# The places of the second layer's input tiles in a scheduled attention and two-layer kernel

## The chip, the cores and the metric

The kernel runs on one core of one Trainium2 chip. The metric is device time in microseconds (us) of one execution. A core has five engines that work side by side, each from its own queue of instructions: TensorE multiplies matrices into PSUM banks, VectorE and ScalarE work element by element, GpSimd is hardly used here, and SyncE (SP) issues the transfers (DMAs) between the chip's memory and SBUF. An instruction whose input is not there yet waits at the head of its engine's queue.

## The reference

Attention over 4 batches, 8 heads, 576 positions and 64 dimensions comes first: half of the heads look at the last 32 positions, the other half at every fourth of the last 128. Its output, put together as 2304 tokens of 512 numbers, goes through two layers without bias, in float32 (each layer has its own weights, 512 x 2048 and 2048 x 512; all four are taken as float64):

```
x = attention(q, k, v)                          # 2304 x 512
h = x @ moe_w_in;  x = (h * sigmoid(1.702 * h)) @ moe_w_out
h = x @ moe2_w_in; r = max(h, 0); out = (r * r) @ moe2_w_out
```

## The kernel before, in words

Tokens lie along the free dimension of a tile, features along its 128 partitions. Every float32 operand of a layer is split into a high part, rounded to float32r, and a low part, the rest; a product is three matmuls (high by high, high by low, low by high).

The tokens are worked off in blocks: six in the first layer (512, 256, 384, 512, 256, 384 columns, `sizes1`), five in the second (512, 256, 512, 512, 512, `BLOCKS2` at line 61). For each block, `step` runs 16 steps f, one for each 128 hidden features. A step has 12 matmuls into a bank h (lines 581 to 583, four pieces k of the input x), the activation (first layer lines 605 to 623; second layer a ReLU on ScalarE, line 633, and a square on VectorE, line 636), the split of its result g into gh (a cast, line 643, on ScalarE or VectorE) and gl (a subtraction on VectorE, line 647), and 12 matmuls into four output banks o (lines 667 to 669). After the last step the banks are evicted (line 690) and stored (line 697), the first layer's into a scratch tensor x2d in the chip's memory.

The input tile of a block holds high and low part of its 512 features. In the first layer it is written by the attention, into one of three places x0, x1, x2 by turns (x0 for blocks 0 and 3, x1 for 1 and 4, x2 for 2 and 5); x1 has room for 256 columns. In the second layer each block's input is filled from x2d (lines 811 to 832): four loads of one piece each (line 817) into a ring of three buffers raw2, and for each piece a cast into the high half (line 823, ScalarE or VectorE) and a subtraction into the low half (line 826, VectorE). These tiles lie in place x0 or in a further place xx, opened when the attention's buffers are given up. A raw2 buffer comes free with its piece's subtraction. In the trace tiles of x0, x1 and x2 have the name x, raw and raw2 buffers the name raw, and copies and subtractions stand at the helpers' lines 234, 236 and 245.

The weights of both layers come as float64 and are turned into split float32 by a chain on ScalarE and VectorE (lines 289 to 318). Each has one place, so the second layer's are made while the first layer's last block runs, step by step as it gives the first layer's up.

The order of all this is written by a planner, the class `Schedule` (lines 64 to 181), when the kernel is built. It holds a cost for every task, plans a start for each, and hands out tasks in the order of these starts; each engine's queue is then fixed, whatever the real times are. A task can start when its predecessors are done, its engine is free and its buffers have a place; at equal start the smaller due time (`want`) goes first (line 143). The place is asked for only as long as no earlier task has taken it for the same buffer:

```
for b in t["bufs"]:
    if not b["held"]:
        ...
        start = max(start, sorted(self.places[c])[k])
...
key = (max(start, free[e] + 0.02) + worse, t["want"], t["n"])
```

Line 158's filling matmuls aside, nothing keeps TensorE running when its next input is late. Due times of the second layer: a block begins where the one before it ends by the planner's costs (lines 743 to 746), step f is due f step lengths later, and piece k of a block's fill is due 60 - 10 k planner's us before the block begins (line 828).

Of the kernel before, what the change touches and what calls it, by code (L numbers as in the profile page):

```python
# [9 lines left out]
F32R = mybir.dt.float32r  # L10
# [7 lines left out]
P = 128  # L18
# [4 lines left out]
KD = DM // P  # L23
# [40 lines left out]
class Schedule:  # L64
# [18 lines left out]
    def buffer(self, cls):  # L83
        return {"cls": cls, "held": False, "left": 0, "end": 0.0}

    def task(self, engine, cost, want, fn, after=(), bufs=(), port=False):


        many = isinstance(engine, tuple)
        t = {  # L90
            "ways": dict(zip(engine, cost)) if many else {engine: cost}, "many": many,
            "want": want, "fn": fn, "bufs": bufs, "port": port,
            "left": 0, "ready": [], "next": [], "n": len(self.tasks), "end": None,
        }
        for a in after:
            a["next"].append(t)
            t["left"] += 1
        for b in bufs:
            b["left"] += 1
        self.tasks.append(t)  # L100
        return t
# [83 lines left out]
def attention_mlp_mlp(  # L185
# [46 lines left out]
    def copy(e, out, in_):  # L232
        if e == "act":
            A.copy(out, in_)  # L234
        else:
            by_name[e].tensor_copy(out, in_)
# [7 lines left out]
    def minus(e, out, a, b):  # L244
        by_name[e].tensor_tensor(out=out, in0=a, in1=b, op=ALU.subtract)  # L245


    def copies(n):
        return ("act", "dve"), (0.19 + n / 1536, 0.068 + n / 1920)
# [4 lines left out]
    def pairs(n):  # L254
        return ("dve",), (0.069 + n / 960,)
# [20 lines left out]
    def weights(layer, f, part, want):  # L276
# [46 lines left out]
        t = task("dve", 0.602, want - LEAD[1], top, [t], [raw_b, c_b], True)  # L323
        t = task("dve", 0.602, want - LEAD[1], low, [t], [raw_b, c_b], True)
        hi = task(*copies(DM), want - LEAD[2], high_part, [t], [c_b, w_b], True)
        lo = task(*pairs(DM), want - LEAD[2], low_part, [hi], [c_b, w_b], True)
        split_task[layer, f, part] = [hi, lo]
# [235 lines left out]
    def step(layer, blk, f, want, a=0, z=None):  # L563
# [81 lines left out]
        def low_part(e):  # L645
            m["gl"] = gpool.tile([P, 512], F32R, tag="gl", name="gl")[:, 0:n]
            minus(e, m["gl"], m["g"], m["gh"])

        hi = task(*copies(n), want, high_part, [last], [g_b, gh_b], True)
        lo = task(*pairs(n), want, low_part, [hi], [g_b, gh_b, gl_b], True)  # L650
        if f == 0:
# [101 lines left out]
    for b in range(1, B):  # L753
# [4 lines left out]
        blk = att_blocks[b - 1]  # L758
# [13 lines left out]
    def step_len(size):  # L772
        return 24 * mm(size)
# [6 lines left out]
    for n, size in enumerate(sizes1):  # L780
        blk = {
            "i": n, "n": size, "c0": sum(sizes1[:n]), "buf": x_buf[n],
            "x": lambda n=n: x_t[n], "ready": lambda k, n=n: x_done[n, k],
        }
# [15 lines left out]
    for n, size in enumerate(BLOCKS2):  # L800
        c0 = sum(BLOCKS2[:n])
        want = begin2[n]
        cls = ("xx", "x0")[n % 2]
        blk = {"i": n, "n": size, "c0": c0, "buf": buffer(cls), "done": {}}
        blk["x"] = lambda blk=blk: blk["tile"]
        blk["ready"] = lambda k, blk=blk: blk["done"][k]
        need = [
            i for i, size1 in enumerate(sizes1)
            if sum(sizes1[:i]) < c0 + size and sum(sizes1[:i]) + size1 > c0
        ]  # L810
        for k in range(KD):
            raw_b = buffer("raw2")
            m = {}

            def load(k=k, c0=c0, size=size, m=m):
                m["raw"] = close["pool"].tile([P, 512], F32, tag="raw2", bufs=3, name="raw2")[:, 0:size]
                nc.sync.dma_start(m["raw"], x2d[k, :, c0:c0 + size])

            def high_part(e, k=k, size=size, m=m, blk=blk, cls=cls):
                if "tile" not in blk:  # L820
                    pool = close["pool"] if cls == "xx" else xpool
                    blk["tile"] = pool.tile([P, 2, KD, 512], F32R, tag=cls, name=cls)
                copy(e, blk["tile"][:, 0, k, 0:size], m["raw"])

            def low_part(e, k=k, size=size, m=m, blk=blk):
                minus(e, blk["tile"][:, 1, k, 0:size], m["raw"], blk["tile"][:, 0, k, 0:size])

            w = want - 60 + 10 * k
            t = task("dma", size * 0.00142, w - 6, load, [stored[0, i, k] for i in need] + [reopened], [raw_b])
            t1 = task(*copies(size), w, high_part, [t], [raw_b, blk["buf"]], True)  # L830
            t2 = task(*pairs(size), w, low_part, [t1], [raw_b, blk["buf"]], True)
            blk["done"][k] = [t1, t2]
        for f in range(KF):
            w = want + step_len(size) * f
            if n == len(BLOCKS2) - 1 and f == KF - 1 and size == 512:

                step(1, blk, f, w, 0, size // 2)
                step(1, blk, f, w + step_len(size // 2), size // 2, size)
            else:
                step(1, blk, f, w)  # L840
# [88 lines left out]
```

## Time and profile before

| | us |
|---|---|
| median of 3 runs | 914.81 (912.86 to 916.9) |
| the profiled execution | 917.75 |
| its span, first to last instruction | 915.9 |
| TensorE busy in it | 890.4 |
| VectorE busy | 553.1 |
| ScalarE busy | 449.6 |

Times inside a trace count from the span's start. The profiled execution is one of its own, so a sum over the trace is made against its 917.75 us. Busy times of TensorE are modelled; its idle times and the starts of its matmuls show where it stood. The second layer begins at about 503 us.

### The profile page before, as it was taken

To read this page: it belongs to the slowest core of one execution; us is meant where nothing else is said; L and a number is where in the kernel's file an instruction comes from. 1 tells how busy PE (TensorE), PEld (TensorE's weight loads), DVE (VectorE), ACT (ScalarE), POOL (GpSimd) and SP (SyncE) were. 2 spreads that over 40 slices of the span, in tenths; PEclk is the share of its full clock that TensorE was granted. 3 is DMA by queue.
4 is the path that set the end of the run, shared out by engine and by line. 5 is a ranking of instruction groups with operands and counts; after the bars stand their busy time and mean duration, and the time that the engine had idled before them with its cause. 6 is when DMAs were issued, how large, how long until landed. Compare 5 with 4: busy or idle time off the path is not lost.

```text
span 915.9 us, 14046 instructions
## 1 busy us (share of the span) xinstructions
PE 890.4 (97%) x5149; PEld 761.0 (83%) x5149; DVE 553.1 (60%) x1542; ACT 449.6 (49%) x1224; POOL 1.2 (0%) x7
## 2 busy tenths in 40 slices
PE   7999999999999999999999999989999999999998
PEld 4677767999988777799999778879888888888887
DVE  6999999766688877764799982232322242222223
ACT  7999898573556555543566642222322232222222
POOL 0000000000000000000000000000000000000000
PEclk9999999999999999999999999989999999999999
DMA  6554445411112110130144520020200010001001
GB/s 232 176 183 158 168 141 169 138 29 40 38 46 79 46 45 23 35 116 1 70 160 146 179 103 0 1 93 1 70 0 1 1 58 1 0 1 46 1 1 46
DMA packets 28117, 65.08 MB, mean 71 GB/s; under 512 B 3121, under 2 KB 10801, under 8 KB 28049
## 3 DMA queue, kind: packets, MB, share of 16 engines
q1 hardware_dynamic: 28048, 64.20, 21.1%
q8 instruction: 40, 0.66, 0.3%
q14 instruction: 29, 0.23, 0.1%
HBM read 54.75 MB, written 9.44 MB: 70 GB/s over the span
## 4 chain that ended last, share of the span: by engine, by line
PE 78%; ACT 9%; DVE 8%; DMA 3%; issue 1%; SPq 0%; ACTq 0%; DVEq 0%
PE o L667 13%; PE o L669 13%; PE o L668 13%; PE h L581 13%; PE h L583 12%; PE h L582 12%; DMA raw<-in_w 2%; ACT sm L468 2%; ACT sm L240 2%; PE s L445 2%; PE pv L537 1%; DVE c L307 1%; ACT c L240 1%; DVE wl L245 1%; DVE c L301 1%
## 5 line engine op out<-in xcount | busy, mean ns | idle before, releaser
L667 PE MATMUL o<-gh,wh 128*128 128x512 f32 (+2 forms) x704 | 250.7, 356 | 6.7 <-ACT gh L234 4.6
L668 PE MATMUL o<-gh,wl 128*128 128x512 f32 (+2 forms) x704 | 248.4, 353 | 1.0 <-DVE wl L245 1.0
L669 PE MATMUL o<-gl,wh 128*128 128x512 f32 (+2 forms) x704 | 248.7, 353 | 0.4 <-DVE gl L245 0.4
L581 PE MATMUL h<-x,wh 128*128 128x512 f32 (+2 forms) x512 | 178.3, 348 | 1.7 <-ACT wh L234 0.9
L583 PE MATMUL h<-x,wl 128*128 128x512 f32 (+2 forms) x512 | 172.9, 338 | 0.9 <-DVE wl L245 0.8
L582 PE MATMUL h<-x,wh 128*128 128x512 f32 (+2 forms) x512 | 172.6, 337 | 0.0
L636 DVE TENSOR_TENSOR g<-g 128x512 f32<-128x512 f32 (+1 forms) x81 | 51.2, 633 | 190.3 <-ACT g L633 189.7
L667 PEld LDWEIGHTS o<-gh,wh 128*128 128x128 f32 x704 | 134.2, 191 | 25.0 <-ACT gh L234 5.2
L668 PEld LDWEIGHTS o<-gh,wl 128*128 128x128 f32 x704 | 134.0, 190 | 17.2 <-DVE wl L245 2.4
L669 PEld LDWEIGHTS o<-gl,wh 128*128 128x128 f32 x704 | 133.8, 190 | 17.4 <-DVE gl L245 2.0
L633 ACT ACTIVATE g<-h 128x512 f32<-128x512 f32 (+1 forms) x81 | 44.6, 550 | 199.2 <-PE h L583 198.4
L234 ACT CAST gh<-g 128x512 fp32r<-128x512 f32 (+2 forms) x166 | 90.4, 544 | 105.6 <-DVE g L636 54.1
L245 DVE TENSOR_TENSOR gl<-g,gh 128x512 fp32r<-128x512 f32 (+2 forms) x177 | 104.2, 589 | 62.9 <-ACT gh L234 58.5
L581 PEld LDWEIGHTS h<-x,wh 128*128 128x128 f32 x512 | 96.9, 189 | 15.5 <-ACT e L610 1.5
L583 PEld LDWEIGHTS h<-x,wl 128*128 128x128 f32 x512 | 97.1, 190 | 9.5 <-DVE wl L245 1.7
L582 PEld LDWEIGHTS h<-x,wh 128*128 128x128 f32 x512 | 97.0, 190 | 7.1 <-DVE x L553 0.4
L606 ACT ACTIVATE g<-h 128x512 f32<-128x512 f32 (+2 forms) x96 | 47.0, 489 | 72.3 <-PE h L583 68.0
L468 ACT ACTIVATE sm<-sm,st 96x128 f32<-96x128 f32 x180 | 70.6, 396 | 15.2 <-DVE st L461 15.2
L582 PE MATMUL h<-xx,wh 128*128 128x512 f32 (+1 forms) x196 | 75.5, 385 | 0.0
L583 PE MATMUL h<-xx,wl 128*128 128x512 f32 (+1 forms) x196 | 75.5, 385 | 0.0
L581 PE MATMUL h<-xx,wh 128*128 128x512 f32 (+1 forms) x196 | 75.4, 385 | 0.0
L620 DVE SCALAR_TENSOR_TENSOR g<-g,h 128x512 f32<-128x512 f32 (+2 forms) x96 | 52.8, 550 | 15.8 <-ACT g L614 10.1
(71 smaller groups left out, 938.1 us busy)
## 6 DMA issues: line engine op xcount, KB each, us to landing
raw<-in_w SPq DMA_DIRECT2D x64, 512.0 KB, 3.5
qk<-in_qkv SPq DMA_DIRECT2D x32, 304.0 KB, 2.9
v<-in_qkv SPq DMA_DIRECT2D x32, 192.0 KB, 2.3
raw<-x2d SPq DMA_DIRECT2D x16, 256.0 KB, 2.7
out_T<-ost SPq DMA_DIRECT2D x14, 256.0 KB, 2.0
x2d<-ost SPq DMA_DIRECT2D x8, 256.0 KB, 3.8
x2d<-ost SPq DMA_DIRECT2D x8, 192.0 KB, 1.9
x2d<-ost SPq DMA_DIRECT2D x8, 128.0 KB, 1.7
```

What stands on the lines that cost most here:

```text
L234: A.copy(out, in_)
L245: by_name[e].tensor_tensor(out=out, in0=a, in1=b, op=ALU.subtract)
L468: A.activation(out=m["sm", j][:, i], in_=m["sm", j][:, i], func=AF.Exp, bias=m["st"][:, 0, j, i:i + 1], scale=-1.0, accum_out=m["st"][:, 1 ...
L581: T.matmul(out, w_hi[:, ks], x[:, 0, k, a:z], start=(k == 0), stop=False)
L582: T.matmul(out, w_hi[:, ks], x[:, 1, k, a:z], start=False, stop=False)
L583: T.matmul(out, w_lo[:, ks], x[:, 0, k, a:z], start=False, stop=(k == KD - 1))
L606: A.activation(out=g(), in_=h(), func=AF.Tanh, scale=0.851)
L620: V.scalar_tensor_tensor(out=g(), in0=g(), scalar=1.0, in1=h(), op0=ALU.add, op1=ALU.mult)
L636: by_name[e].tensor_tensor(out=g(), in0=g(), in1=g(), op=ALU.mult)
L667: T.matmul(out, w_hi[:, ds_], m["gh"], start=(f == 0 or extra), stop=False)
L668: T.matmul(out, w_lo[:, ds_], m["gh"], start=False, stop=False)
L669: T.matmul(out, w_hi[:, ds_], m["gl"], start=False, stop=(f == KF - 1))
```

## The change

Only the place of the second layer's input tiles changes. Blocks 0 to 4 lie in xx, x0, xx, x0, xx before, and in xx, x1, x0, xx, x0 after. The tile in x1 is allocated with 256 columns, as the first layer does there; it is block 1, which has 256.

```
-        cls = ("xx", "x0")[n % 2]
+        cls = ("xx", "x1", "x0", "xx", "x0")[n]
         blk = {"i": n, "n": size, "c0": c0, "buf": buffer(cls), "done": {}}
...
                 if "tile" not in blk:
                     pool = close["pool"] if cls == "xx" else xpool
-                    blk["tile"] = pool.tile([P, 2, KD, 512], F32R, tag=cls, name=cls)
+                    blk["tile"] = pool.tile([P, 2, KD, 256 if cls == "x1" else 512], F32R, tag=cls, name=cls)
```

## Rows read from the trace of the kernel before

**Rows 1.** The page's busy time, share of the span and instructions: TensorE.

```profile
PE 890.4 (97%) x5149; PEld 761.0 (83%) x5149; DVE 553.1 (60%) x1542; ACT 449.6 (49%) x1224; POOL 1.2 (0%) x7
```

**Rows 2.** Stretches: length, each engine's busy us (instructions), clock, DMA share, GB/s.

```profile
600.00:700.00 100.00, 97.91 (x587) 88.06 (x588) 32.27 (x63) 27.97 (x59) 0.00 (x0) 0.97 0.10 32
```

**Rows 3.** TensorE's waits in the whole span: total us, times, longest.

```profile
PE o L667 <- ACT gh L234: 4.6, 2, 3.6
```

**Rows 4.** Timeline from block 0's last step: start, duration, engine, operation, idle before.

```profile
589.32 0.39 PE L667 MATMUL o<-gh,wh 128*128 128x512 f32 x1
...
592.04 0.39 PE L667 MATMUL o<-gh,wh 128*128 128x512 f32 x1
...
594.76 0.28 PE L581 MATMUL h<-x,wh 128*128 128x256 f32 x1
...
594.96 0.62 ACT L234 CAST xx<-raw 128x512 fp32r<-128x512 f32 x1 [6.12 <-PE h L583]
594.96 0.76 DVE L236 CAST xx<-raw 128x512 fp32r<-128x512 f32 x2 [5.39 <-PE h L583]
...
595.49 0.59 ACT L633 ACTIVATE g<-h 128x512 f32<-128x512 f32 x1
...
595.64 1.28 DVE L245 TENSOR_TENSOR xx<-raw,xx 128x512 fp32r<-128x512 f32 x2
...
596.35 4.78 SPq L817 DMA_DIRECT2D raw<-x2d  x4
...
598.26 0.28 PE L583 MATMUL h<-x,wl 128*128 128x256 f32 x1
599.03 0.43 DVE L236 CAST xx<-raw 128x512 fp32r<-128x512 f32 x1 [2.11 <-DMA raw<-x2d]
...
600.70 1.02 DVE L636 TENSOR_TENSOR g<-g 128x512 f32<-128x512 f32 x2
601.42 0.62 ACT L234 CAST gh<-g 128x512 fp32r<-128x512 f32 x1 [4.65 <-DVE g L636]
...
602.09 0.79 PE L667 MATMUL o<-gh,wh 128*128 128x512 f32 x1 [3.56 <-ACT gh L234]
...
607.38 0.30 PE L667 MATMUL o<-gh,wh 128*128 128x256 f32 x1
```

**Rows 5.** Stretches, columns as in rows 2: one microsecond after the wait.

```profile
603.00:604.00 1.00, 1.00 (x4) 0.80 (x4) 0.52 (x2) 0.47 (x2) 0.00 (x0) 0.50 0.02 8
```

**Rows 6.** Timeline at the end of block 2, where block 4 fills xx.

```profile
731.51 0.39 PE L581 MATMUL h<-x,wh 128*128 128x512 f32 x1
...
731.77 0.60 ACT L633 ACTIVATE g<-h 128x512 f32<-128x512 f32 x1 [0.74 <-PE h L583]
...
732.40 0.69 DVE L636 TENSOR_TENSOR g<-g 128x512 f32<-128x512 f32 x1
...
734.22 0.69 DVE L245 TENSOR_TENSOR gl<-g,gh 128x512 fp32r<-128x512 f32 x1
...
736.30 0.43 DVE L236 CAST xx<-raw 128x512 fp32r<-128x512 f32 x1 [0.79 <-DMA raw<-x2d]
```

**Rows 7.** Timeline where the first layer's block 4 ends and block 5 begins.

```profile
435.68 0.44 PE L581 MATMUL h<-x,wh 128*128 128x384 f32 x1
...
438.69 0.43 DVE L245 TENSOR_TENSOR gl<-g,gh 128x256 fp32r<-128x256 f32 x1 [0.53 <-ACT gh L234]
...
439.17 0.28 PE L667 MATMUL o<-gh,wh 128*128 128x256 f32 x1
...
442.05 0.42 DVE L242 TENSOR_SCALAR ost<-o 128x256 f32<-128x256 f32 x1 [2.94 <-DMA x2d<-ost]
```

**Rows 8.** Stretches, columns as in rows 2: first layer's block 5.

```profile
440.00:442.00 2.00, 2.00 (x15) 2.00 (x14) 0.00 (x0) 0.48 (x2) 0.00 (x0) 1.00 0.39 131
...
490.00:500.00 10.00, 10.00 (x59) 10.00 (x59) 10.00 (x22) 5.65 (x11) 0.00 (x0) 1.00 0.35 123
```

**Rows 9.** Fills of x places: durations in ns (min/median/max), first and last start.

```profile
L245 DVE TENSOR_TENSOR x<-raw,x x8: 418/555/694, 393.4 to 652.3; 128x256 fp32r<-128x256 f32 x4, 128x512 fp32r<-128x512 f32 x4
```

## The prediction

> **What bounds the kernel now.** I read the page's busy shares first: TensorE is busy 97% of the span [rows 1], so only its idle time and time at a low clock can be won. The stretches by 100 us come next: in the one from 600 to 700, deep in the second layer, TensorE is idle for 2.1 us and the mean granted clock is 0.97 [rows 2]. The list of TensorE's waits says where to look: its longest single wait of the whole run is 3.6 us, for the activation's high part (gh, made by ScalarE), and it lies in the second layer [rows 3].
>
> The timeline around it shows the cause [rows 4]. Block 0 of the second layer ends its first products at 594.76, where block 1's begin. Block 2's input goes into the same place xx, so its casts wait for that moment: ScalarE stands 6.12 us and VectorE 5.39 us before them. VectorE then does two casts and two subtractions, and next in its queue is the cast of the fourth piece, whose load could be issued only at 596.35, when a raw2 buffer came free; VectorE stands another 2.11 us for it. Behind that cast and two more subtractions, at 600.70, stands the square of block 0's last step, which ScalarE had ready before 596.1. So gh starts at 601.42 and TensorE, whose last matmul before the hole began at 598.26, resumes at 602.09 after 3.56 us idle. [...] The place costs 3.56 + 2.57 = 6.1 us.
>
> **Why the queue stands like that.** The order is the planner's. Lines 132 to 140 ask when a place is free only for a buffer not yet held. Block 2's first cast is due 87.0 + 46.1 - 60 = 73 planner's us after block 0 begins (its lines 828 and 746; mm gives 5.44 for a 512 step), block 0's last ReLU 15 x 5.44 = 82. So ScalarE gets the cast at the moment xx comes free, the buffer is then held, and VectorE, whose planned time is earlier because it was idle, gets the other casts and subtractions at a time when xx is not free in fact. They land in its queue ahead of the square.
>
> **The change part by part.** No instruction is added or removed; the four fills with 512 columns and the one with 256 keep their casts, subtractions and loads. What moves is when each can run.
>
> Block 2 now goes into x0, last read by the first layer's block 3, so it no longer waits for 594.76. What is left at that moment is block 3's fill into xx. Its due time is 87 later, 160 after block 0's beginning, against 82 for the ReLU; at equal start the smaller due time wins, so ScalarE takes the ReLU first, VectorE takes the first cast itself at the true time, and no later piece can be planned before it. The trace has this case: block 4's fill into xx at the end of block 2, due 114 against 82 [rows 6]. There the ReLU starts at 731.77, the square at 732.40 ahead of the subtractions, and gl is done at 734.22 + 0.69 = 734.91, 3.40 us after the next block's first matmul at 731.51; the cast of the fourth piece waits 0.79 us and TensorE not at all. Carried to 594.76 it makes gl at 598.16, and TensorE has matmuls until 598.26 + 0.28 = 598.54. The next steps are 256 columns wide, so VectorE gets their squares in between: cost from 0 to one subtraction in front, 0.6 us; I take 0.3. Term: -6.1 + 0.3. The fill that ends at 652.3 now, block 3's, goes away there [rows 9].
>
> Block 1 goes into x1, which the first layer's block 4 reads until block 5 begins at 435.68. Its fill moves there from 393.4 and after [rows 7, 9], and its raw2 buffers are kept until then, so block 2's loads follow only after it. VectorE has room: after 438.69 + 0.43 it idles until the eviction at 442.05, 2.94 us, and in 440 to 442 it does nothing [rows 7, 8]. Four subtractions of 0.42 us [rows 9] and four casts, no longer than those, fit partly there, partly between block 4's last steps. What they may delay is block 4's last gl, which ends at 439.12, 0.05 us before the matmul at 439.17 that follows it. Bounds: below, 0, and even a few tenths won, since the fill leaves the busy place at 393; above, all eight in front of it, 8 x 0.42 = 3.4 us. I take 0.3, nearer the idle row, since the due times put the last steps ahead of the fill in every tie.
>
> Block 2's fill follows: four subtractions at 0.64 (1.28 for two in rows 4) and four casts at 0.38 on VectorE or about 0.6 on ScalarE. About two pieces fit before 442; the rest comes in a stretch where VectorE is full, 10.00 of 10 us in 490 to 500, and TensorE also [rows 8]. Due later than every weight split, they are taken where the plan has a hole. Bounds: 0 to 4 x 0.64 + 4 x 0.38 = 4.1 us, if VectorE sets the pace. TensorE still works without a gap there, so I take half of two subtractions at most, 0.3.
>
> The five loads (block 1's last, block 2's four) now stand in SP's queue beside block 4's stores of about 440; the eviction at 442.05 already waits for such a store [rows 7]. Bounds: 0 to as much again, 2.9 us; I take 0.2, since ScalarE and TensorE have other work there. Block 4's fill takes x0 instead of xx, at the end of block 2 as before: 0, covered by the same 2.7 us steps as in rows 6.
>
> Sum: -6.1 + 0.3 + 0.3 + 0.3 + 0.2 = -5.0 us. The profiled execution took 917.75 (span 915.9), so it would take 912.7; it lies 2.9 above the median of the runs, 914.81, and the same difference gives 909.8.
>
> [...]
>
> **Rivals.** (a) The stall stays: block 3's fill meets the same place, the same four pieces and three raw2 buffers, and if its fourth cast is again ahead of the square the 6.1 us are paid again. For it: the place and moment are unchanged. Against it: the due times and rows 6. Time 914.8, or with the 0.8 of the other terms 915.6.
> (b) It shrinks, but TensorE still waits once, 1.5 us for a fourth piece in front of block 1's short steps, and half of the clock loss stays, 1.3. For it: the margin at 598.2 is only 0.4 us. Time 909.8 + 2.8 = 912.6.
> (c) Slower: the wait moves to 436 and costs more. Casts for x1 wait at the head of ScalarE's and VectorE's queues, the fourth piece's load has to land (2.1 us of VectorE's time in rows 4) with block 4's last steps behind it; TensorE pays a stall of 3.6 and the clock's 2.6, and VectorE, full until past 500, cannot make up its lost 2.1 and the 4.1 of block 2's fill: 12.4 against the 6.1 saved, 921.1. It decides where more than 6.1 us are lost between 436 and 510. For it: the 0.05 us margin and the full VectorE. Against it: VectorE is busy shortly before x1 comes free, so the plan has no early time to misplace pieces into.
>
> **How the numbers follow.** About 0.5%, 4.6 us, is what a measurement of this kernel can tell from no change. Forecast 64%, own range 907.5 to 911.8; (a) 12%, 914.8 to 915.6; (b) 14%, 912.6; (c) 10%, up to 921. Below 910.2 lie some 52 of the forecast's 64 hundredths, since its added terms lean to small costs, and 3 of (b): faster 0.55. Slower by more than 4.6 us is most of (c), 0.08. The rest is 0.37. The range takes the forecast with all four added terms at zero and a microsecond of scatter, 907, less one more for the shorter waits that other queue orders may leave, 906, and reaches up past (a) to 916.
>
> **What would show it.** TensorE's list of waits without the 3.6 us for gh, and a full clock in 600 to 610; block 2's casts between 439 and 510; block 3's at about 595 behind the ReLU, the square before its subtractions; no fill around 650 and block 4's at about 727. I am wrong if a cast into the new xx is followed on VectorE by a wait for a load and then a square, or if new idle time of TensorE stands between 436 and 510.

## The result and the profile after

The changed kernel takes 906.42 us (median of 4 runs, 905.04 to 906.98) against 914.5 (912.86 to 916.9): a ratio of 0.9907, 95% interval 0.9882 to 0.9933, so 8.1 us less. In a second study on another chip it was 907.36 against 916.16, 0.9903 (0.9886 to 0.992). The forecast was 5.0 us less.

The profiled execution took 905.95 us, 11.8 less than the one of before. Of these 1.7 have nothing to do with the change: up to block 4 of the first layer, which begins at 386.61 before and 384.95 after, the queues of TensorE, VectorE and ScalarE are the same. The profile of before has a stretch at half speed there, among the attention's work: the granted clock is 0.50 from 123 to 126 and 0.98 in 100 to 200, where after it is 1.00. The page's busy line, in the columns of [rows 1] (six casts have moved from VectorE to ScalarE):

```profile
PE 884.1 (98%) x5149; PEld 758.6 (84%) x5149; DVE 551.5 (61%) x1536; ACT 453.5 (50%) x1230; POOL 1.2 (0%) x7
```

TensorE's waits in the whole span, as [rows 3]: the 3.6 us for gh are gone, and the longest that are left lie in the attention (s) or are an eviction's.

```profile
PE s L445 <- DMA qk<-in_qkv: 2.6, 2, 1.8
PE s L445 <- DVE st L482: 2.0, 1, 2.0
PE s L445 <- DVE x L553: 1.7, 1, 1.7
PE o L667 <- ACT ost L240: 1.3, 2, 1.0
```

Stretches, as [rows 2]: full clock and no idle time from 600 to 700, and 0.09 us of idle time in the 10 us behind block 0.

```profile
600.00:700.00 100.00, 100.00 (x592) 89.35 (x592) 27.58 (x51) 25.80 (x53) 0.00 (x0) 1.00 0.02 7
590.00:600.00 10.00, 9.91 (x72) 9.22 (x71) 6.34 (x13) 5.30 (x12) 0.00 (x0) 1.00 0.62 202
```

The timeline where block 0 ends and block 1 begins answers to [rows 4]; what fills xx here is block 3.

```profile
588.96 0.28 PE L581 MATMUL h<-x,wh 128*128 128x256 f32 x1
...
589.16 0.76 DVE L236 CAST xx<-raw 128x512 fp32r<-128x512 f32 x2 [5.40 <-PE h L583]
589.22 0.60 ACT L633 ACTIVATE g<-h 128x512 f32<-128x512 f32 x1 [6.18 <-PE h L583]
...
589.71 0.61 ACT L234 CAST xx<-raw 128x512 fp32r<-128x512 f32 x1
589.85 0.69 DVE L636 TENSOR_TENSOR g<-g 128x512 f32<-128x512 f32 x1
590.46 1.29 DVE L245 TENSOR_TENSOR xx<-raw,xx 128x512 fp32r<-128x512 f32 x2
590.58 0.62 ACT L234 CAST gh<-g 128x512 fp32r<-128x512 f32 x1 [0.25 <-DVE g L636]
...
591.66 0.69 DVE L245 TENSOR_TENSOR gl<-g,gh 128x512 fp32r<-128x512 f32 x1
...
592.55 0.40 PE L667 MATMUL o<-gh,wh 128*128 128x512 f32 x1
```

VectorE waits for xx just as long as before, 5.40 us, but behind its two casts comes the square, at 589.85; ScalarE waits 6.18 us, now for the last h of block 0, whose ReLU it does first. The product with gh starts at 592.55, 3.6 us after block 1's first matmul, where it was 602.09 - 594.76 = 7.3. Order and distances are those of [rows 6].

The timeline at the first layer's block 4 to 5, as [rows 7]: block 1's fill into x1 waits for it, block 2's first pieces follow into x0.

```profile
434.23 0.34 PE L581 MATMUL h<-x,wh 128*128 128x384 f32 x1
434.43 0.50 DVE L236 CAST x<-raw 128x256 fp32r<-128x256 f32 x2 [0.23 <-PE h L583]
...
437.42 0.41 ACT L234 CAST x<-raw 128x256 fp32r<-128x256 f32 x1 [0.38 <-DMA raw<-x2d]
...
439.31 1.14 ACT L234 CAST x<-raw 128x512 fp32r<-128x512 f32 x2
...
441.53 0.68 DVE L245 TENSOR_TENSOR x<-raw,x 128x512 fp32r<-128x512 f32 x1
442.20 0.42 DVE L242 TENSOR_SCALAR ost<-o 128x256 f32<-128x256 f32 x1
```

The eviction, which VectorE awaited for 2.94 us before, now stands at 442.20 behind other work, and VectorE has no hole there, as the stretches that answer to [rows 8] show (VectorE's busy time is the third of the five):

```profile
440.00:442.00 2.00, 2.00 (x14) 2.00 (x13) 2.00 (x5) 1.41 (x4) 0.00 (x0) 1.00 0.68 227
490.00:500.00 10.00, 10.00 (x59) 9.91 (x58) 10.00 (x20) 7.38 (x16) 0.00 (x0) 1.00 0.51 174
```

**Where TensorE's time went.** A busy share cannot show short pauses, since a matmul's recorded time (0.28 to 0.39 us) is longer than the distance to the next one. So the pauses were counted from the starts: for each pair of neighbouring matmuls the distance, less what it is on average in an undisturbed stretch of these traces (0.1199 us behind one of 256 columns, 0.1733 behind 384, 0.2266 behind 512), summed from one block's first matmul to the next block's. In us, for all profiles of this study:

| kernel | layer 1, block 4 | layer 1, block 5 | layer 2, block 0 | layer 2, block 1 | sum |
|---|---|---|---|---|---|
| before | 1.91 | 0.96 | 2.96 | 6.34 | 12.17 |
| after | 0.68 | 0.01 | 1.01 | 0.39 | 2.09 |
| after, second study | 0.72 | 0.01 | 1.53 | 0.33 | 2.59 |
| block 2's fill due later | 2.51 | 0.98 | 2.04 | 0.09 | 5.62 |
| the same, second study | 2.80 | 0.98 | 1.43 | 0.18 | 5.39 |
| planner mended | 2.68 | 0.98 | 1.57 | 0.69 | 5.92 |
| after, block 3's fill due early | 0.79 | 0.01 | 1.26 | 7.07 | 9.13 |
| block 1 in x1, block 2 in xx | 0.28 | 4.64 | 0.28 | 0.48 | 5.68 |
| after, block 1 in x2 | 0.73 | 0.85 | 0.68 | 0.06 | 2.32 |
| after, block 2's loads late | 0.78 | 4.56 | 0.76 | 0.60 | 6.70 |

Blocks 2 to 4 of the second layer lose 0.1 us together, in the last three kernels of the table 0.7. The change takes away 5.95 us in block 1, which is the stall, and 4.13 in the three blocks ahead of it, which the prediction had put down as a loss of 0.8.

### The profile page after: what moved, and what is told of

Its sections match the earlier page's. It is cut to its first block, busy times and chain, and to the rows that moved or that the text cites. A ratio compares the mean times of both kernels' runs of the same rounds, so it can differ in the third digit from the quotient of the medians.

```text
span 904.2 us, 14039 instructions
## 1 busy us (share of the span) xinstructions
PE 884.1 (98%) x5149; PEld 758.6 (84%) x5149; DVE 551.5 (61%) x1536; ACT 453.5 (50%) x1230; POOL 1.2 (0%) x7
## 4 chain that ended last, share of the span: by engine, by line
PE 82%; ACT 8%; DVE 6%; DMA 3%; issue 1%; SPq 0%; ACTq 0%; DVEq 0%
PE o L667 13%; PE h L581 13%; PE o L669 13%; PE o L668 13%; PE h L583 13%; PE h L582 13%; PE s L445 2%; ACT sm L240 1%; ACT sm L468 1%; PE pv L537 1%; DMA raw<-in_w 1%; DMA x2d<-ost 1%; DVE c L301 1%; DVE c L307 1%; ACT g L606 1%; ACT c L240 1%
## 5 line engine op out<-in xcount | busy, mean ns | idle before, releaser
L581 PE MATMUL h<-x,wh 128*128 128x512 f32 (+2 forms) x580 | 202.7, 350 | 0.8 <-ACT e L610 0.6
L583 PE MATMUL h<-x,wl 128*128 128x512 f32 (+2 forms) x580 | 198.4, 342 | 0.8 <-DVE wl L245 0.8
L582 PE MATMUL h<-x,wh 128*128 128x512 f32 (+2 forms) x580 | 198.0, 341 | 0.0
L234 ACT CAST gh<-g 128x512 fp32r<-128x512 f32 (+2 forms) x170 | 92.5, 544 | 106.8 <-DVE g L636 50.5
L581 PEld LDWEIGHTS h<-x,wh 128*128 128x128 f32 x580 | 109.6, 189 | 15.0 <-ACT e L610 1.2
L583 PEld LDWEIGHTS h<-x,wl 128*128 128x128 f32 x580 | 109.8, 189 | 11.9 <-DVE wl L245 1.7
L582 PEld LDWEIGHTS h<-x,wh 128*128 128x128 f32 x580 | 109.9, 189 | 9.4 <-DVE x L553 0.4
L623 DVE SCALAR_TENSOR_TENSOR g<-e,g 128x512 f32<-128x512 f32 (+2 forms) x96 | 53.1, 553 | 1.1
L583 PE MATMUL h<-xx,wl 128*128 128x512 f32 x128 | 49.8, 389 | 0.0
L582 PE MATMUL h<-xx,wh 128*128 128x512 f32 x128 | 49.8, 389 | 0.0
```

What stands on the lines that cost most here:

```text
L581: T.matmul(out, w_hi[:, ks], x[:, 0, k, a:z], start=(k == 0), stop=False)
L582: T.matmul(out, w_hi[:, ks], x[:, 1, k, a:z], start=False, stop=False)
L583: T.matmul(out, w_lo[:, ks], x[:, 0, k, a:z], start=False, stop=(k == KD - 1))
L623: V.scalar_tensor_tensor(out=g(), in0=m["e"], scalar=1.0, in1=g(), op0=ALU.min, op1=ALU.mult)
```

## The experiments

**Only block 2's due time.** Places as before; the fill of block 2 is due later than block 0's last ReLU.

```
-            w = want - 60 + 10 * k
+            w = want - (40 if n == 2 else 60) + 10 * k
```

> The kernel before with one number changed: the fill of the second layer's block 2 is due 20 planner's us later (first cast due 93 instead of 73 after block 0's beginning, against 82 for block 0's last ReLU); all places stay as before. Theory (the stall after block 0 is a matter of queue order alone): ScalarE takes the ReLU first, VectorE no longer has a cast that waits for a load ahead of the square, TensorE's 3.6 us wait and the half-speed stretch go, block 1 takes about 46.3 us instead of 52.2 from its first matmul to block 2's first, and the whole 914.5 - 6.1 = 908.4. The time from block 4's first matmul (first layer) + the second layer's block 0 to block 1's first matmul stays at about 208.1. Rival (the gain needs block 2 filled early, in x0): 914.5 again, block 1 at 52.

Measured: 910.12 against 917.13, 0.9924 (0.9902 to 0.9947), which is 7.0 us less where 6.1 were expected. Its timeline at the end of block 0, in xx as before:

```profile
592.98 0.76 DVE L236 CAST xx<-raw 128x512 fp32r<-128x512 f32 x2 [5.39 <-PE h L583]
593.67 0.69 DVE L636 TENSOR_TENSOR g<-g 128x512 f32<-128x512 f32 x1
594.27 1.29 DVE L245 TENSOR_TENSOR xx<-raw,xx 128x512 fp32r<-128x512 f32 x2
```

The square moved ahead of the subtractions, block 1 takes 45.97 us instead of 52.22, and the three blocks ahead keep most of their pauses. TensorE's own queue is that of the kernel before, matmul for matmul. To remove the stall, neither an early fill nor another place is needed: it is the order of the queues of VectorE and ScalarE.

**The changed kernel with the stall brought back.**

```
-            w = want - 60 + 10 * k
+            w = want - (160 if n == 3 else 60) + 10 * k
```

> The changed kernel with one number changed: the fill of block 3 into xx is due 100 planner's us earlier (60 after block 0's beginning, before the ReLU's 82). Up to block 0's end the order is the changed kernel's. Theory: ScalarE takes the cast first, VectorE's pieces are planned before xx is free and stand ahead of the square, the stall of 3.6 us and the half-speed stretch are back, block 1 takes about 52 us and the whole 906.4 + 6 = 912.5. Rival (a fill into xx at block 0's end is harmless once block 2 lies elsewhere): 906.4.

Measured: 915.32 against 917.13, 0.9979 (0.9964 to 0.9993). The waits from 585 to 610, and one us after them:

```profile
DVE xx L236 <- PE h L583: 5.4, 1, 5.4
...
PE o L667 <- ACT gh L234: 4.2, 1, 4.2
...
DVE xx L236 <- DMA raw<-x2d: 2.1, 1, 2.1
```

```profile
601.00:602.00 1.00, 1.00 (x4) 0.81 (x3) 0.42 (x1) 0.47 (x2) 0.00 (x0) 0.50 0.10 35
```

The wait of 2.1 us for the fourth piece's load is back, TensorE idles 4.2 us and has a granted clock of 0.50 behind it; block 1 takes 52.95 us. The places of the changed kernel alone do not keep it free of the stall; the due times that come with them do.

**The planner mended.** Due times and places as before; a task on a held buffer also waits for the time at which its place came free.

```
                     for b in t["bufs"]:
-                        if not b["held"]:
+                        if b["held"]:
+                            start = max(start, b["from"])
+                        else:
                             c = b["cls"]
...
-                    self.places[b["cls"]].pop(0)
+                    b["from"] = self.places[b["cls"]].pop(0)
```

> The kernel before with its places and due times as they are; only the planner is mended: a task on a buffer that is already held also waits for the time at which its place came free. Theory (the stall comes from pieces planned on VectorE before xx is free, not from the due time as such): ScalarE still takes block 2's first cast ahead of the ReLU, half a us late, but VectorE's casts stand at their true time and no cast that waits for a load stands ahead of the square; block 1 takes 46 to 47 us, the ratio to before is that of the kernel with the due time changed, 0.993, some 910. Rival (the smaller due time of the fill is enough to put its four pieces ahead of the square): block 1 at 52, ratio 1.0. What block 4, block 5 and block 0 lose stays as before, about 5.5 us together.

Measured: 911.7 against 916.07, 0.996 (0.9941 to 0.9979). Its timelines of ScalarE and of VectorE (two lines of the kernel were added, so 236 stands for 234 and so on):

```profile
594.79 0.62 ACT L236 CAST xx<-raw 128x512 fp32r<-128x512 f32 x1 [6.12 <-PE h L585]
...
595.32 0.59 ACT L635 ACTIVATE g<-h 128x512 f32<-128x512 f32 x1
```

```profile
594.79 0.76 DVE L238 CAST xx<-raw 128x512 fp32r<-128x512 f32 x2 [5.40 <-PE h L585]
595.47 0.68 DVE L247 TENSOR_TENSOR xx<-raw,xx 128x512 fp32r<-128x512 f32 x1
596.08 0.68 DVE L638 TENSOR_TENSOR g<-g 128x512 f32<-128x512 f32 x1
```

ScalarE still does the cast before the ReLU, and VectorE two casts and one subtraction before the square, but nothing that waits for a load stands ahead; block 1 takes 46.57 us. So the smaller due time alone does not make the stall; the pieces that the planner put on VectorE at a time when xx was not yet free do. The whole gained 4.4 us between medians where 6 were expected. The pauses in the profile, 5.92 against 12.17, bear the 6 out; the runs do not, even at the far end of their interval (0.9941 is 5.4 us). The difference stays unexplained.

**Block 1 moved alone.**

```
-        cls = ("xx", "x0")[n % 2]
+        cls = ("xx", "x1", "xx", "x0", "xx")[n]
```

(with the 256-column tile of the change)

> Places xx, x1, xx, x0, xx: block 1 goes to x1 as in the change, block 2 still to xx after block 0, so nothing of block 2 is filled early. Theory (the further 4 us between 386 and 595 come from moving block 1's fill to the first layer's block 4/5 boundary, which also moves block 5's first matmuls and the weights' splits earlier): that stretch takes about 204 as in the changed kernel, not 208. Rival (they come from block 2's early fill and the raw2 buffers it frees): 208. At the end of block 0 the first cast goes ahead of the ReLU on ScalarE by 0.5 us, but VectorE's casts stand at their true time, so at most a short wait of TensorE, under 1.5 us. Whole: theory 906 to 908, rival 910 to 912.

Measured: 911.17 against 917.13, 0.994 (0.992 to 0.996). Neither side is right: the time from block 4's first matmul to block 1's is 204.8 us, near the theory's 204, but only because twelve more of block 0's matmuls (2.7 us) come after block 1's first there; block 4 and block 0 lost their pauses, as the theory had it, and block 5 got 3.7 us more (4.64 against 0.96; the 3.9 that a later expectation gives leave out the pause at the block's end). Its waits of TensorE in block 5:

```profile
PE h L581 <- DVE g L620: 1.3, 3, 0.5
PE h L581 <- ACT e L610: 0.6, 2, 0.3
```

TensorE waits there for a bank h until VectorE's multiplication (line 620) or ScalarE's exponential (line 610) has read it, at two steps out of three; at 475.93 its matmul had stood idle 0.54 us for line 620.

**Block 1 in x2.**

```
-        cls = ("xx", "x1", "x0", "xx", "x0")[n]
+        cls = ("xx", "x2", "x0", "xx", "x0")[n]
```

(its tile with 384 columns)

> Places xx, x2, x0, xx, x0: the change with block 1 in x2 (384 columns), which the first layer's block 5 holds until about 500, so blocks 1 and 2 are filled only after 500, beside the last weight splits; nothing is filled at 435. Theory (the further 4 us need a fill at the block 4/5 boundary, which reorders the work there): of them only about 1 us comes, from the fill that leaves 393, so the stretch from the first layer's block 4 to block 1 takes about 207, and the whole is about 907.5 to 908.5. Rival (the fill's leaving 393 is enough): 204 and 906.4. Second rival (fills beside the last weight splits cost VectorE's time): over 209, whole over 909.5.

Measured: 909.63 against 917.13, 0.9924 (0.9902 to 0.9945). Block 4's pauses fall to 0.73 without any fill at its end, so it is the fill's leaving 393 that frees it. Block 5 keeps 0.85. The stretch from block 4 to block 1 took 201.9 us, with twelve more of block 0's matmuls (2.7 us) behind it than in the changed kernel, so the second rival is out. The two fills beside the last weight splits cost nothing that can be seen: block 0 loses 0.68. In the profile its sum of pauses, 2.32, is near the changed kernel's; yet its runs gained no more than those of the kernel with the due time. Half a us more is lost in the last step of the second layer's block 4; the rest of this difference stays open.

**The changed kernel beside the one with the due time, on one chip.**

> The changed kernel unaltered, on the chip of the two runs beside it. From the first layer's block 4's first matmul to the last matmul of all it takes about 514.7 us, as in its first profile (before 524.8). Theory (the change is worth more than the stall): its time lies 3 to 4 us below that of the kernel with only the due time changed. Rival (the four extra us are scatter of transfers): within 1 us of it.

> The kernel before with only block 2's due time changed, again, beside the changed kernel: about 518.3 us over the same stretch, and a ratio to before of about 0.993; theory 3 to 4 us above the changed kernel, rival within 1 us.

Measured: 907.36 and 910.42 against 916.16, ratios 0.9903 (0.9886 to 0.992) and 0.9932 (0.9915 to 0.995). From block 4's first matmul to the last of all the two profiles take 515.0 and 517.9 us. The stall is worth 5.7 us there, the rest of the change 3.1, and the pauses of the two profiles, 2.59 and 5.39, differ by 2.8. The rival of scatter is out: the six runs of each hardly overlap (906.12 to 909.26, 908.98 to 911.1).

**Block 2's pieces kept out of block 5.**

```
-    t = task("dma", size * 0.00142, w - 6, load, [stored[0, i, k] for i in need] + [reopened], [raw_b])
+    t = task("dma", size * 0.00142, w - 6, load, [stored[0, i, k] for i in need + [5] * (n == 2)] + [reopened], [raw_b])
```

> The changed kernel, but block 2's loads also wait for the first layer's last stores (about 505), so that block 1's fill stays at the boundary of the first layer's blocks 4 and 5 and nothing of block 2 is filled beside block 5. With places xx, x1, xx, x0, xx that fill alone left TensorE 3.9 us idle in block 5 (before 1.0, the changed kernel 0.0) while it took the idle time of block 4 and of the second layer's block 0 away. Theory (the early pieces of block 2 are what keeps block 5 free of waits): TensorE loses 2 to 4 us in block 5 again, 65.3 becomes 67 to 69, and the whole is 2 to 4 us above the changed kernel. Rival (block 1's place alone decides, and the 3.9 belong to block 2's going to xx): block 5 at 65.3 and the whole equal to the changed kernel's.

Measured: 913.93 against 916.16, 0.9967 (0.9953 to 0.9982), 6.6 us above the changed kernel beside it, where the theory had 2 to 4. The pauses of the table make 4.1 of it and the last step of block 4 another 0.5; the rest stays open. Block 5 loses 4.56 us and takes 67.7, as the theory had it; block 4 loses 0.78. The stretch 450 to 500 of this kernel, of the one with block 1 moved alone, and of the changed kernel (the first number in brackets counts TensorE's matmuls):

```profile
450.00:500.00 50.00, 48.09 (x270) 46.19 (x268) 48.05 (x99) 28.28 (x59) 0.00 (x0) 1.00 0.43 138
```

```profile
450.00:500.00 50.00, 48.52 (x271) 46.40 (x269) 48.09 (x98) 31.67 (x64) 0.00 (x0) 1.00 0.46 144
```

```profile
450.00:500.00 50.00, 50.00 (x290) 49.91 (x289) 50.00 (x101) 35.09 (x71) 0.00 (x0) 1.00 0.45 157
```

The kernel of before has 290 matmuls there as well. With block 1's fill at the boundary and nothing of block 2 behind it, VectorE is busy 48.05 us instead of 50.00, and yet TensorE gets 20 matmuls less done: a fuller VectorE is not what holds it up. What does is told below, by the order of TensorE's own matmuls.

## Why the prediction came out as it did

**The stall, its cause and its price: right.** The term was -6.1 + 0.3. Of the 6.1, 2.57 us are those of twelve matmuls of 512 columns behind the wait, which took 5.29 us (602.09 to 607.38) where twelve at the end of block 0 took 2.72 [rows 4], at a granted clock of 0.50 [rows 5]. Block 1 lost 6.34 us before and 0.39 after; the kernel with the due time lost 6.2 less than before in block 1, and the changed kernel with an early due time got 6.7 back. The argument by due times and by lines 132 to 140 holds in both directions, and the mended planner shows that the held buffer is the cause. Rivals (a) and (b) did not come: the fourth cast stands behind the square (on ScalarE, at 593.94), and TensorE's last matmul before the product was followed at once.

**The moved fills: the step that failed.** "I take 0.3, nearer the idle row", "I take half of two subtractions at most, 0.3" and the 0.2 for the loads made 0.8 us of cost. These terms together should have been a gain of 3: on one chip the changed kernel lies 3.1 us below the one that only lacks the stall. No run takes the loads by themselves. By block, taking the kernels with the order of before (four profiles) against the changed one and its copies up to block 0 (three profiles):
- block 4 of the first layer, 1.91 to 2.80 against 0.68 to 0.79: some 1.7 us, because block 1's fill no longer stands at 393 and the order behind it is another one. The prediction gave "even a few tenths won" as the lower bound of its cost. It is shown by all five kernels whose block 1 is not filled there, whatever else they do: 0.28 to 0.79.
- block 5, 0.96 to 0.98 against 0.01: 1.0 us. It needs both parts: with block 1's fill alone it gets worse, to 4.6 in two kernels, with neither it stays, 0.85 with block 1 in x2.
- block 0, 1.43 to 2.96 against 1.01 to 1.53: 0.7 us with much scatter. The kernels with the due time and of before have the same queues up to there and differ by up to 1.5.

**What the moved fills changed.** Not VectorE's load but TensorE's own order, which the planner also writes. The matmuls into h of one step are twelve; where those of nearly three steps follow one another without a product into o between them, the two banks h (line 221) were not enough in the first layer's block 5, and TensorE waited until VectorE's line 620 or ScalarE's line 610 had read one: 1.9 us of idle time at five matmuls with block 1 moved alone, 2.1 us at four with block 2's loads late. Counted from the starts, for the first layer: the longest run of matmuls into h, and the pauses in runs of 30 or more against all of the block, in us.

| kernels | block 4: longest run | in runs of 30 or more, of all | block 5: longest run | in runs of 30 or more, of all |
|---|---|---|---|---|
| before, due later (twice), planner mended | 36 | 1.5 of 1.9 to 2.8 | 36 | 0.9 of 1.0 |
| after (twice), block 3's fill due early | 21 | none of 0.7 to 0.8 | 24 | none of 0.0 |
| after, block 1 in x2 | 21 | none of 0.7 | 30 | 0.83 of 0.85 |
| block 1 in x1, block 2 in xx | 21 | none of 0.3 | 33 | 4.47 of 4.64 |
| after, block 2's loads late | 21 | none of 0.8 | 33 | 4.53 of 4.56 |

So most of block 4's gain comes from steps far behind the fill at 393, through an order that no longer stacks three steps, and block 5 is free of pauses in the changed kernel because it has no such run. In the second layer runs of 39 stand without a pause where there is no stall (the changed kernel's from 586.92 to 592.55), so length alone is not enough: there a ReLU is all that reads a bank h. This is read from the traces; no run changes TensorE's order alone, and why the planner's costs lead to the one order or the other was not followed.

**Why the term had the wrong sign.** The prediction read "TensorE still works without a gap there" from busy shares of 10.00 of 10, and took the moved work as something that could do little but cost. For 490 to 500, the stretch it showed, that is right: the pauses of block 5 stand at 444 to 448. They and those of block 4 were in the trace, 0.05 to 0.4 us long and mostly hidden by the recorded durations: of the 5.8 us that blocks 4, 5 and 0 lose before, only 1.65 show as idle time of TensorE, 1.39 of them in block 0. TensorE's weight loads (PEld) of before waited in 386 to 503

```profile
PEld h L581 <- DVE g L620: 1.2, 5, 0.6
PEld h L581 <- ACT e L610: 0.3, 1, 0.3
```

and those of after, in the same part,

```profile
PEld o L667 <- ACT ost L240: 0.5, 1, 0.5
```

Had the starts been counted, the sum would have begun with some 5.8 us in blocks 4, 5 and 0 that a new order could take away or double, and the lower bound would have lain near 914.8 - 6.1 - 5.8 = 903, not 906.

**The slower rival.** A loss in block 5 exists, 3.6 and 3.7 us more than before in two of the kernels tried. But it comes from TensorE's order and its two banks h, not from a wait at 436 and VectorE's load, as it was worked out, and not with the change as it stands.

## What to carry to other kernels

Where queues are fixed ahead by a planner, look for tasks that it places before their buffer is really free: here one of them waited 2.11 us for its load, with the square behind it in VectorE's queue until 600.70 [rows 4], and mending the order alone took this stall away, with every place as it was. Before a moved piece of work is booked as a cost, count the pauses of the busiest engine from the starts of its instructions against their undisturbed distance; busy shares hid 4.2 of the 5.8 us lost in three blocks. Then look whether steps are stacked in that engine's queue deeper than the buffers they write to. Where a change of places alters the order of a tightly interleaved stretch, its worth cannot be summed from durations: in block 5 the whole change gave -1 us and one part of it alone almost +4.

## What was not expected of the hardware

Executions of one kernel on one chip spread over 5.5 us (913.67 to 919.19 for 17 runs of the kernel before), and the granted clock over the span goes with it: its two runs at 919 have 0.990, those below 916 have 0.993 to 0.995. A short stretch at half speed in the attention may be part of that: in 120 to 140 the granted clock is 0.91 (before: 0.50 from 123 to 126) in eight of the ten profiles and 1.00 in the two of the changed kernel, though the queues of TensorE, VectorE and ScalarE are the same there in all ten. What decides it was not found. A single profile of each kernel therefore gave 11.8 us where the runs gave 8.1.
